# Attention values in lent PSUM banks of a feed-forward product, and softmax inverses spread in place, in a fused Linformer kernel

## The chip, the cores and the metric

The kernel runs on one core of one Trainium2 chip. The metric is the device time of one execution in microseconds (us), as the median of several runs. Five engines work side by side and meet through semaphores: TensorE (PE in the profile; PEld are its weight loads), VectorE (DVE), ScalarE (ACT), GpSimd (POOL) and SyncE (SP), which issues most DMAs here.

## The reference

A Linformer attention is followed by a feed-forward layer with a squared relu. There are 8 batches, 8 heads, 1024 tokens, a head width of 64, and keys and values are projected along the tokens to length 64; the feed-forward layer has widths 512, 2048, 512.

```python
k_proj = np.einsum('ks,bhsd->bhkd', E, k)          # E, F: 64 x 1024
v_proj = np.einsum('ks,bhsd->bhkd', F, v)
scores = (1 / sqrt(64)) * q @ k_proj^T             # 1024 x 64 per head
attn   = softmax(scores)                           # over the 64
x      = attn @ v_proj, heads side by side         # 8192 x 512
h      = np.maximum(x @ w_in, 0.0)                 # 8192 x 2048
out    = (h * h) @ w_out                           # 8192 x 512, float32
```

## The kernel before, in words

**The feed-forward part.** A batch is cut into two chunks of 512 tokens. For each chunk both feed-forward products are computed with a Strassen scheme (Winograd's form): seven half-size products in place of eight, with sums of the inputs made beforehand (`sum_x`, `sum_h`, and the sums of the weights). The first product is worked off in four `Group`s (g = 0 to 3) per chunk. A group has seven steps in the order `p1, p5, p4` (of the group before), `p6, p2, p3, p7`, each of four matmuls of 256 columns, written at line 669. It uses the PSUM banks `bank0` to `bank3`: `first` is bank 1, `other` is bank 2, and `chain` is bank 3 for even g and bank 0 for odd g.

```python
self.first, self.chain = bank(n=turn["bank"] + 1), bank(n=turn["bank"] + 3 + self.g % 2)
```

`p1` fills `first`, and ScalarE copies it to `chain` (L694). `p6` adds to `chain`, `p2` adds to `first`, and a relu on ScalarE (L679) takes each out when it is complete; for `other` (after `p3`) and for `chain` after `p7` a relu of a sum on VectorE does it (`relu_sum`, L683). So `first` lies free from the relu after `p2` until the next group's `p1`, and the chain bank of the group before lies free from the relu after its `p4` until ScalarE's copy after the next group's `p1`.

The second product of the chunk before runs between these steps (`second_spread`, L583): one step of the first product, then one quantum of four matmuls of the second, in its own two banks. Its product 1 ends with a copy of one bank to the other on ScalarE (L599); one step has no quantum and the next has two.

**The attention part.** The attention of the next batches is planned into these steps. Heads go in pairs; there are four pairs a batch, pr = 0 to 3. All of attention shares one pair of PSUM banks (`ps_att`, from `att_psum`). Per pair of heads:

- `scores` (L339): two matmuls of 512 columns, then an exponential on ScalarE (L353) to `expT`.
- `sums_spread` for two pairs at once (L392): eight matmuls on 64x32 tiles of the array with ones as weights; then ScalarE makes the inverse as exp(-ln(sum)) (L396, L397) in the tile `inv`. Each sum stands in 32 partitions, and the scaling needs it in 64. DMAs on SyncE (L403) copy it, 32 partitions of 4 KB each, to two places of a tile `rs` per pair of heads: eight DMAs in all. `inv` and `rs` come from a pool of three buffers.
- `values` (L415): four matmuls of 512 columns on the four 64x64 tiles of the array, into the two halves of `ps_att`; then VectorE multiplies each half by `rs` into `xT` (L419). `xT` is the input of the first product, and `sum_x` makes its sums.

**What sets the order.** TensorE's order is written out by hand: `run` counts steps, and `at` or `on` hangs a stage of attention behind a step. Steps count from 1; a chunk has 28, a batch 56, and `t = 56 * (b - 1) + 28` is the end of the first chunk of batch b, so that t+1 is `p1` of group 0 of its second chunk, t+6 is `p3` and t+7 `p7` of group 0, t+8 `p1` of group 1, t+20 `p3` of group 2, and t+22 `p1` of group 3. At t+6 there is no quantum of the second product, and at t+7 there are two. The other engines follow the order in which a scheduler places their instructions; `tc.issue_after(x)` puts an instruction behind x in it. The load of Q for the batch after next (GpSimd, L89) waits for the scaling of pair 1.

Of the kernel before, what the change touches and what calls it, by code (L numbers as in the profile page):

```python
# [9 lines left out]
P = 128  # L10
F32 = mybir.dt.float32
BF16 = mybir.dt.bfloat16
AF = mybir.ActivationFunctionType
# [6 lines left out]
def kernel(  # L20
# [11 lines left out]
    nc = tc.nc  # L32
# [12 lines left out]
    TCH = S // 2  # L45
# [15 lines left out]
    soft_pool = ctx.enter_context(tc.tile_pool(name="soft", bufs=3))  # L61
# [5 lines left out]
    turn = {"att": 0, "bank": 0, "step": 1, "pairs": 2}  # L67

    lent = ctx.enter_context(ExitStack())
# [5 lines left out]
    def att_psum(shape=(P, 2, TCH), dtype=F32):  # L75
        turn["att"] += 1
        return pair_psum(turn["att"] % turn["pairs"], shape, dtype)

    def bank(shape=(P, 512), dtype=F32, n=None):
        if n is None:  # L80
            turn["bank"] += turn["step"]
            n = turn["bank"]
        return psum.tile(list(shape), dtype, tag=f"bank{n % 4}", name="ps_bank")
# [48 lines left out]
    for j, (lo, hi) in enumerate(W_IN_PIECES):  # L132
        t = wpool.tile([P, NCB, (hi - lo) * P], BF16, name=f"w_in_{lo}")
# [7 lines left out]
    for j in range(WP):  # L141
        t = wpool.tile([P, fn, DM], BF16, name=f"w_out_{j}")
# [89 lines left out]
    class Attention:  # L232
# [153 lines left out]
        def sums_spread(self, pr):  # L386

            ps = att_psum()
            for j in range(2):
                for o, par, a, r in VALUE_QUADS:  # L390
                    c = 32 * (2 * a + j)
                    nc.tensor.matmul(  # L392
                        ps[c:c + 32, par], lhsT=ones[r, 0:32], rhs=self.e[pr + j][r, a], start=True, stop=True
                    )
            inv = soft_pool.tile([P, 2, TCH], F32, tag="rs", name="inv")
            nc.scalar.activation(inv[:], ps[:], AF.Ln)  # L396
            nc.scalar.activation(inv[:], inv[:], AF.Exp, scale=-1.0)  # L397
            for j in range(2):
                rs = soft_pool.tile([P, 2, TCH], F32, tag="rs", name="rs")
                for a in range(2):  # L400
                    have = 32 * (2 * a + j)
                    for to in (64 * a, 64 * a + 32):
                        nc.sync.dma_start(rs[to:to + 32], inv[have:have + 32])  # L403
                self.rs[pr + j] = rs

        def values(self, pr, spare=False):

            e, rs = self.e.pop(pr), self.rs.pop(pr)
            if spare:
                ps_x = [bank(), bank()]  # L410
            else:
                ps = att_psum()
                ps_x = [ps[:, par] for par in range(2)]
            for o, par, a, r in VALUE_QUADS:
                nc.tensor.matmul(  # L415
                    ps_x[par][o], lhsT=self.vp[r, 2 * pr + a, :], rhs=e[r, a], start=True, stop=True
                )
            for par in range(2):
                self.done = nc.vector.tensor_tensor(  # L419
                    out=self.xT[:, pr, :, par], in0=ps_x[par].rearrange("p (c t) -> p c t", c=2),  # L420
                    in1=rs[:, par].rearrange("p (c t) -> p c t", c=2), op=ALU.mult,
                )


        def chunk_scores(self, c, g):
# [234 lines left out]
    class Group:  # L660
# [19 lines left out]
            self.square(kh, a)  # L680

        def relu_sum(self, kh, a, ps, more):
            nc.vector._custom_dve(TENSOR_ADD_SAT, out=self.out(kh, a), in0=ps[:], in1=more[:], s0=3.0e38, s1=0.0)  # L683
            self.square(kh, a)

        def square(self, kh, a):
# [38 lines left out]
    with tc.manual_schedule(engines={PE}):  # L725
# [33 lines left out]
        def at(step, fn, *args, **kwargs):  # L759
            plan.setdefault(step, []).append(lambda: fn(*args, **kwargs))  # L760
# [110 lines left out]
        def on(step, b, name, *args):  # L871
            at(step, lambda: getattr(atts[b], name)(*args))
# [5 lines left out]
        for b in range(B - 1):  # L878
            t = 56 * (b - 1) + 28
            if b:  # L880
                on(t + 1, b + 1, "scores", 3)
                on(t + 3, b + 1, "sums_spread", 2)
                on(t + 7, b + 1, "values", 0)
                on(t + 10, b + 1, "values", 1)
                on(t + 20, b + 1, "values", 2)
                on(t + 23, b + 1, "values", 3)
                at(t + 24, lambda b=b: chunk[b + 1, 0].sum_x())
            at(t + 51, lambda b=b: chunk[b + 1, 1].sum_x())
            if b + 2 < B:
                if b:  # L890
                    on(t + 11, b + 2, "load_q", lambda b=b: atts[b + 1].done)
                on(t + (26 if b else 32), b + 2, "transpose_q_dma")
                on(t + (28 if b else 36), b + 2, "project")
                on(t + (30 if b else 37), b + 2, "transpose_k_dma")
                if b + 3 < B:
                    at(t + (32 if b else 37), begin, b + 3)
                    on(t + (32 if b else 37), b + 3, "load_kv", lambda b=b: atts[b + 2].kT_done)
                on(t + (44 if b else 45), b + 2, "scores", 0)
                on(t + (47 if b else 48), b + 2, "scores", 1)
                on(t + (50 if b else 51), b + 2, "sums_spread", 0)  # L900
                on(t + (53 if b else 54), b + 2, "scores", 2)
# [34 lines left out]
```

The softmax here doesn't subtract the row's maximum and nothing guards it: scores larger than these inputs give would overflow.

## Time and profile before

| | before |
|---|---|
| median of 5 runs | 473.03 us (472.68 to 475.01) |
| profiled execution, its own time | 473.03 us |
| its span, first to last instruction | 471.2 us |
| TensorE, VectorE, ScalarE busy | 465.3, 348.1, 297.7 us |
| one period of 56 steps (a batch) | 55.33 us |
| matmul pieces at L669 and L583 on the chain that ended last | 37% and 36% |
| DMAs `rs<-inv` (L403) | 96, of 128 KB each, median 2.3 us to landing |

A row of a timeline has the start in us from the span's start, the length in us, engine, source line, operation, the tile written and the tiles read; for matmuls then the tile of the array and the moving operand's shape, the number of like instructions in a row, and in brackets the idle time before and what ended it. A matmul's length goes up to its modelled end, so that runs of matmuls overlap in these rows; the distance between starts is the time that TensorE spends.

### The profile page before, as it was taken

To read this page: it belongs to the slowest core of one execution; us is meant where nothing else is said; L and a number is where in the kernel's file an instruction comes from. 1 tells how busy PE (TensorE), PEld (TensorE's weight loads), DVE (VectorE), ACT (ScalarE), POOL (GpSimd) and SP (SyncE) were. 2 spreads that over 40 slices of the span, in tenths; PEclk is the share of its full clock that TensorE was granted. 3 is DMA by queue.
4 is the path that set the end of the run, shared out by engine and by line. 5 is a ranking of instruction groups with operands and counts; after the bars stand their busy time and mean duration, and the time that the engine had idled before them with its cause. 6 is when DMAs were issued, how large, how long until landed. Compare 5 with 4: busy or idle time off the path is not lost.

```text
span 471.2 us, 10124 instructions
## 1 busy us (share of the span) xinstructions
PE 465.3 (99%) x4141; PEld 367.2 (78%) x4141; DVE 348.1 (74%) x596; ACT 297.7 (63%) x484; POOL 34.0 (7%) x47
## 2 busy tenths in 40 slices
PE   8999999999999999999999999999999999999997
PEld 4544677788888787887888888888878878888886
DVE  2469985876968779667895679777796778968571
ACT  3488595887467863687556775568736875565641
POOL 7430100100010000100001000100000000000000
PEclk9999999999999999999999999999999999999999
DMA  9999998995879578785979849695692154101012
GB/s 181 201 205 206 161 199 187 173 223 111 170 151 210 144 134 202 127 171 130 175 183 145 170 105 177 154 195 156 108 209 89 32 132 106 68 24 68 24 69 89
DMA packets 85743, 67.90 MB, mean 144 GB/s; under 512 B 34368, under 2 KB 82240, under 8 KB 85696
## 3 DMA queue, kind: packets, MB, share of 16 engines
q0 software_dynamic: 32208, 29.23, 41.0%
q1 hardware_dynamic: 53488, 38.02, 30.2%
q8 instruction: 32, 0.52, 0.5%
q14 instruction: 15, 0.12, 0.1%
HBM read 59.24 MB, written 16.78 MB: 161 GB/s over the span
## 4 chain that ended last, share of the span: by engine, by line
PE 97%; DMA 1%; DVE 1%; issue 0%; ACT 0%; POOL 0%; DVEq 0%; POOLq 0%
PE ps_bank L669 37%; PE ps_second L583 36%; PE ps_bank L502 6%; PE ps_bank L562 4%; PE ps_att L339 3%; PE ps_att L270 3%; PE ps_att L415 2%; PE ps_second L562 1%; DMA Q_sb<-in_q_dram 1%; PE ps_att L392 1%; PE ps_bank L314 1%; PE ps_att L349 1%; PE ps_att L345 1%; PE ps_att L289 0%; PE ps_bank L220 0%; DVE qT L318 0%
## 5 line engine op out<-in xcount | busy, mean ns | idle before, releaser
L154 DVE TENSOR_TENSOR h<-h 128x1024 bf16<-128x1024 bf16 (+1 forms) x170 | 105.4, 646 | 43.9 <-ACT h L679 38.7
L669 PE MATMUL ps_bank<-x_sum,w_in_sum 128*128 128x256 bf16 x672 | 101.1, 273 | 0.0
L669 PEld LDWEIGHTS <-w_in_sum 128*128 128x128 bf16 x896 | 85.3, 98 | 19.0 <-issue 6.3
L583 PEld LDWEIGHTS <-h 128*128 128x128 bf16 x896 | 87.4, 98 | 10.8
L683 DVE CUSTOM_DVE_ANT_0 h<-ps_bank,u 128x512 bf16<-128x512 f32 x112 | 73.8, 685 | 16.3 <-PE ps_bank L669 12.1
L557 ACT COPY u<-ps_bank 128x512 f32<-128x512 f32 x115 | 68.0, 591 | 24.9 <-PE ps_bank L669 23.7
L694 ACT COPY ps_bank<-ps_bank 128x512 f32<-128x512 f32 x56 | 32.0, 571 | 81.5 <-PE ps_bank L669 81.5
L679 ACT ACTIVATE h<-ps_bank 128x512 bf16<-128x512 f32 x112 | 67.9, 607 | 16.7 <-PE ps_bank L669 15.8
L669 PEld LDWEIGHTS <-w_in 128*128 128x128 bf16 x672 | 64.2, 98 | 14.6 <-issue 5.2
L583 PEld LDWEIGHTS <-s 128*128 128x128 bf16 x672 | 65.7, 98 | 7.7
L669 PE MATMUL ps_bank<-xT,w_in 128*128 128x256 bf16 x448 | 67.3, 273 | 0.0
L583 PE MATMUL ps_second<-w_out_sum,s 128*128 128x256 bf16 x448 | 67.3, 273 | 0.0
L583 PE MATMUL ps_second<-w_out_sum,h 128*128 128x256 bf16 x448 | 67.1, 273 | 0.0
L583 PE MATMUL ps_second<-w_out,h 128*128 128x256 bf16 x448 | 64.7, 273 | 0.0
L419 DVE TENSOR_TENSOR xT<-ps_att,rs 128x512 bf16<-128x512 f32 x48 | 30.9, 685 | 13.7 <-PE ps_att L415 13.7
L353 ACT ACTIVATE expT<-ps_att 128x1024 bf16<-128x1024 f32 x32 | 33.1, 1034 | 5.3 <-PE ps_att L339 5.0
L154 DVE TENSOR_TENSOR o_sb<-ps_second,u 128x512 f32<-128x512 f32 x29 | 19.9, 685 | 19.3 <-PE ps_second L583 13.6
L669 PE MATMUL ps_bank<-x_sum,w_in 128*128 128x256 bf16 x224 | 33.7, 273 | 0.0
L669 PE MATMUL ps_bank<-xT,w_in_sum 128*128 128x256 bf16 x224 | 33.6, 273 | 0.0
L583 PE MATMUL ps_second<-w_out,s 128*128 128x256 bf16 x224 | 33.6, 273 | 0.0
L502 PE MATMUL ps_bank<-xT,w_in 128*128 128x512 bf16 x128 | 29.2, 380 | 0.0
L557 ACT COPY u<-ps_second 128x512 f32<-128x512 f32 x30 | 17.6, 585 | 11.6 <-PE ps_second L583 9.3
(96 smaller groups left out, 461.8 us busy)
## 6 DMA issues: line engine op xcount, KB each, us to landing
out_dram<-o_sb SPq DMA_DIRECT2D x63, 256.0 KB, 2.5
rs<-inv SPq DMA_DIRECT2D x96, 128.0 KB, 2.3
K_sb<-in_k_dram POOLq DMA_DIRECT2D x7, 1024.0 KB, 10.1
V_sb<-in_v_dram POOLq DMA_DIRECT2D x7, 1024.0 KB, 14.7
Q_sb<-in_q_dram POOLq DMA_DIRECT2D x6, 1024.0 KB, 12.0
w_out<-in_moe_w_out_dram POOLq DMA_DIRECT2D x4, 512.0 KB, 15.9
Q_sb<-in_q_dram POOLq DMA_DIRECT2D x4, 256.0 KB, 11.0
V_sb<-in_v_dram POOLq DMA_DIRECT2D x2, 512.0 KB, 11.0
```

The source lines that it names most:

```text
L154: return nc.vector.tensor_tensor(out=o, in0=x, in1=y, op=op)
L270: nc.tensor.matmul(ps[LO, 0], lhsT=ET[:, i, :], rhs=self.K[:, :, i, :], start=f, stop=l)
L353: self.done = nc.scalar.activation(e[:], ps[:], AF.Exp, scale=SCALE)
L419: self.done = nc.vector.tensor_tensor(out=self.xT[:, pr, :, par], in0=ps_x[par].rearrange("p (c t) -> p c t", c=2), in1=rs[:, par].rearran ...
L502: nc.tensor.matmul(ps[:], lhsT=w_in_blk(cb, fb), rhs=self.xT[:, cb, self.c].rearrange("p a t -> p (a t)"), start=(cb == 0), stop=(cb == NC ...
L557: nc.scalar.copy(u[:], ps)
L562: nc.tensor.matmul(ps[:, i * HM:(i + 1) * HM], lhsT=self.h_form(n, fb)[:, i * P:(i + 1) * P], rhs=w_out_form(n, fb), start=fresh and fb == ...
L583: nc.tensor.matmul(ps[:, i * HM:(i + 1) * HM], lhsT=self.h_form(n, fb)[:, i * P:(i + 1) * P], rhs=w_out_form(n, fb), start=fresh and i == ...
L669: nc.tensor.matmul(ps[:, j * HC:(j + 1) * HC], lhsT=w_in_form(n, cb, 2 * self.g + j), rhs=self.chunk.x_form(n, cb), start=fresh and j == 0 ...
L679: nc.scalar.activation(self.out(kh, a), ps[:], AF.Relu)
L683: nc.vector._custom_dve(TENSOR_ADD_SAT, out=self.out(kh, a), in0=ps[:], in1=more[:], s0=3.0e38, s1=0.0)
L694: nc.scalar.copy(self.chain[:], self.first[:])
```

## The change

In the six batches b = 1 to 6 of the plan (they compute the attention of batches 2 to 7):

- The sums of pairs 2 and 3 move from t+3 to t+6, and the values of pair 0 from t+7 to t+6, behind them.
- The values of pair 2 stay at t+20; the matmuls of pair 3's values move from t+23 to t+20, behind them, and their scaling to t+21.
- The values of pairs 0 and 2 go to bank 1 and bank 0 of the first product (`values_lent`); those of pairs 1 and 3 stay in `ps_att`. VectorE's relu-sum after `p7` of that group is put behind the scaling of the lent banks.
- The inverse is made in the first of the two `rs` tiles, so that there is no tile `inv`: four DMAs fill the second tile, then two complete the first in place, six instead of eight.

```diff
-            inv = soft_pool.tile([P, 2, TCH], F32, tag="rs", name="inv")
-            nc.scalar.activation(inv[:], ps[:], AF.Ln)
-            nc.scalar.activation(inv[:], inv[:], AF.Exp, scale=-1.0)
-            for j in range(2):
-                rs = soft_pool.tile([P, 2, TCH], F32, tag="rs", name="rs")
+            rs = [soft_pool.tile([P, 2, TCH], F32, tag="rs", name="rs") for _ in range(2)]
+            nc.scalar.activation(rs[0][:], ps[:], AF.Ln)
+            nc.scalar.activation(rs[0][:], rs[0][:], AF.Exp, scale=-1.0)
+            for j in (1, 0):
                 for a in range(2):
                     have = 32 * (2 * a + j)
                     for to in (64 * a, 64 * a + 32):
-                        nc.sync.dma_start(rs[to:to + 32], inv[have:have + 32])
-                self.rs[pr + j] = rs
-
-        def values(self, pr, spare=False):
-
-            e, rs = self.e.pop(pr), self.rs.pop(pr)
-            if spare:
-                ps_x = [bank(), bank()]
-            else:
+                        if j or to != have:
+                            nc.sync.dma_start(rs[j][to:to + 32], rs[0][have:have + 32])
+                self.rs[pr + j] = rs[j]
+
+        def values_products(self, pr, lent):
+            ps_x = [bank(n=turn["bank"] + n)[:] for n in (1, 4)] if lent else None
+            if not lent:
                 ps = att_psum()
                 ps_x = [ps[:, par] for par in range(2)]
+            e = self.e.pop(pr)
             for o, par, a, r in VALUE_QUADS:
                 nc.tensor.matmul(
                     ps_x[par][o], lhsT=self.vp[r, 2 * pr + a, :], rhs=e[r, a], start=True, stop=True
                 )
+            self.ps_x[pr] = ps_x
+
+        def scale(self, pr):
+            ps_x, rs = self.ps_x.pop(pr), self.rs.pop(pr)
             for par in range(2):
                 self.done = nc.vector.tensor_tensor(
                     out=self.xT[:, pr, :, par], in0=ps_x[par].rearrange("p (c t) -> p c t", c=2),
                     in1=rs[:, par].rearrange("p (c t) -> p c t", c=2), op=ALU.mult,
                 )
+            return self.done
+
+        def values(self, pr):
+            self.values_products(pr, False)
+            self.scale(pr)
+
+        def values_lent(self, pr):
+            self.values_products(pr, True)
+            turn["lent"] = self.scale(pr)
...
         def relu_sum(self, kh, a, ps, more):
-            nc.vector._custom_dve(TENSOR_ADD_SAT, out=self.out(kh, a), in0=ps[:], in1=more[:], s0=3.0e38, s1=0.0)
+            with ExitStack() as order:
+                if (kh, a) == (1, 1) and "lent" in turn:
+                    order.enter_context(tc.issue_after(turn.pop("lent").ins))
+                nc.vector._custom_dve(TENSOR_ADD_SAT, out=self.out(kh, a), in0=ps[:], in1=more[:], s0=3.0e38, s1=0.0)
             self.square(kh, a)
...
                 on(t + 1, b + 1, "scores", 3)
-                on(t + 3, b + 1, "sums_spread", 2)
-                on(t + 7, b + 1, "values", 0)
+                on(t + 6, b + 1, "sums_spread", 2)
+                on(t + 6, b + 1, "values_lent", 0)
                 on(t + 10, b + 1, "values", 1)
-                on(t + 20, b + 1, "values", 2)
-                on(t + 23, b + 1, "values", 3)
+                on(t + 20, b + 1, "values_lent", 2)
+                on(t + 20, b + 1, "values_products", 3, False)
+                on(t + 21, b + 1, "scale", 3)
                 at(t + 24, lambda b=b: chunk[b + 1, 0].sum_x())
```

## The prediction

> **What bounds the kernel now.** I read the busy shares first, then the granted clock, the waits of TensorE, and TensorE's own timeline through one batch.
>
> ```profile
> PE 465.3 (99%) x4141; PEld 367.2 (78%) x4141; DVE 348.1 (74%) x596; ACT 297.7 (63%) x484; POOL 34.0 (7%) x47
> PEclk9999999999999999999999999999999999999999
> PE ps_bank L220 <- DVE zeros L123: 1.2, 1, 1.2
> PE ps_bank L211 <- DVE e_bf L727: 0.5, 1, 0.5
> PE ps_att L339 <- DVE kT L301: 0.4, 2, 0.2
> PE ps_bank L278 <- ACT K_sb L728: 0.3, 1, 0.3
> 151.83:207.16 55.33, 55.33 (x506) 45.46 (x505) 42.96 (x73) 35.58 (x60) 2.62 (x3) 1.00 0.79 161
> ```
>
> TensorE is busy for 99% of the span at full clock. Its four listed waits come to 2.4 us, all before 61 us, outside the stretches that the change touches. The last line is one period of 56 steps: 55.33 us, TensorE busy throughout. So whatever TensorE time disappears moves the end, unless a wait takes its place. The change removes no matmul; it can gain only where matmuls stand closer together.
>
> ```profile
> 161.92 0.60 PE L583 MATMUL ps_second<-w_out,h 128*128 128x256 bf16 x4
> 162.36 0.60 PE L669 MATMUL ps_bank<-xT,w_in_sum 128*128 128x256 bf16 x4
> 162.80 0.60 PE L669 MATMUL ps_bank<-x_sum,w_in_sum 128*128 128x256 bf16 x4
> 163.26 1.03 PE L583 MATMUL ps_second<-w_out,h 128*128 128x256 bf16 x8
> 164.22 0.41 PE L415 MATMUL ps_att<-expT,vp 64*64 64x512 bf16 x4
> 164.57 0.61 PE L669 MATMUL ps_bank<-xT,w_in 128*128 128x256 bf16 x4
> ```
>
> Each row is a run of matmuls: start, length, tile of the array. Full-array runs of four start 0.437 us apart. The eight from 163.26 need 0.875, so they end streaming at 164.13; values start at 164.22, and the next full-array run at 164.57. The four values matmuls (four different 64x64 quarters, all four inside 0.41 us where one alone takes 0.40) therefore cost 0.44 us of TensorE.
>
> ```profile
> 184.35 0.40 PE L270 MATMUL ps_att<-K_sb,ET 128*64 128x512 bf16 x1
> 184.59 0.38 PE L270 MATMUL ps_att<-K_sb,ET 128*64 128x512 bf16 x1
> 184.81 0.38 PE L270 MATMUL ps_att<-K_sb,ET 128*64 128x512 bf16 x1
> ```
>
> These are 512-column matmuls that follow each other with no change of tile shape: 0.24 us to the second, 0.22 to the third. So of the 0.44 about 0.215 is streaming, and 0.22 is paid for changing shape twice: 0.11 us a change. The sums (64x32) cost the same: 160.60 less the end of streaming before them (159.73 + 0.437) is 0.43.
>
> **The change, part by part.** It acts in six batches (b = 1 to 6; the trace has 24 blocks of values and 12 of sums).
>
> *Place A, t+6.* The sums of pairs 2 and 3 move from t+3 to t+6 and the values of pair 0 from t+7 to t+6, right behind them. Two lone blocks have four changes of shape; adjacent they have three: into 64x32, to 64x64, out. The trace has no change between two small shapes. Bounds: it is free (gain 0.22), or as dear as a way out and in (gain 0). I take one ordinary change, 0.11, as both small shapes cost alike against the full array: gain 0.11.
>
> [...]
>
> *Place B, t+20.* Values of pair 3 move from t+23 next to values of pair 2. Same shape, so two changes go: 0.22, less up to 0.02 for the first follower (0.24 instead of 0.22 above). I take 0.21.
>
> *A small wait.* At 163.26 the run starts 0.03 late (162.80 + 0.437 = 163.23): it waits for ScalarE's copy of the second bank (L599, 162.62 to 163.21). With the sums behind it, the last matmul of t+5 ends 0.43 earlier and the copy at about 162.8, while TensorE needs it at about 163.6. Gain 0.03.
>
> *The lent banks.* Values of pairs 0 and 2 now write the bank of `first` and the bank that odd groups use as `chain`. Three new meetings follow.
>
> (1) Values wait for ScalarE's relu of product 2 on bank 1. At B product 2 ends streaming at 175.07; relu ran 175.27 to 175.87 and values would start at 176.47: 0.6 spare. At A the relu comes at 161.7 to 162.3, values at 162.79: 0.5 spare. Cost 0.
>
> (2) Product 1 of the next group, two steps on, waits for the first half of the scaling. The order of the built program has this wait on the first of the two VectorE multiplies. VectorE starts 0.47 us after the first values matmul (164.69 against 164.22), a half takes 0.69, and a released TensorE starts 0.04 later.
>
> ```profile
> 176.35 0.68 DVE L683 CUSTOM_DVE_ANT_0 h<-ps_bank,u 128x512 bf16<-128x512 f32 x1
> 176.95 1.28 DVE L419 TENSOR_TENSOR xT<-ps_att,rs 128x512 bf16<-128x512 f32 x2
> 162.02 0.69 DVE L154 TENSOR_TENSOR s<-h,s 128x1024 bf16<-128x1024 bf16 x1
> 163.10 1.29 DVE L683 CUSTOM_DVE_ANT_0 h<-ps_bank,u 128x512 bf16<-128x512 f32 x2 [0.39 <-PE ps_bank L669]
> ```
>
> At B the first half is done at 176.95 + 0.69 + 0.04 = 177.68; product 1 stood at 177.70 and comes 0.22 later, behind the second block: 0.24 spare. (In one batch VectorE starts this scaling 0.25 later: nothing spare, nothing lost.) At A: product 3 streams from 161.92, sums from 162.45, values from 162.79; the relu-sum of product 3 follows the subtraction that ends at 162.71 and takes until about 163.35; first half done about 164.05, given back 164.09. Product 1 comes after product 7 and the two second-product runs of t+7, at 162.79 + 0.34 + 0.437 + 0.875 = 164.44: 0.35 spare. Cost 0, cover thin at both. ScalarE's copy into the other lent bank comes after product 1 (165.05 at A) and the second half ends at 164.7. Cost 0.
>
> (3) The relu-sum of product 7 now stands behind the scaling on VectorE: at A it ends at about 165.3, where product 4 wants the bank at 166.2. At B nothing moves (it stands there already). The scaling of pair 3 gets earlier, from 180.0 to about 179.4. Cost 0.
>
> *Spreading in place.* Per pair of pairs 6 DMAs of 128 KB replace 8, on SyncE, which is not on the path: no gain. But pair j=0's two now wait until j=1's have read their source, and in the program the sixth stands behind an output store. Who waits for it is VectorE's scaling, behind that TensorE. Rows of the second batch: the exponential ends at about 165.0, DMAs 1 to 4 go out from 165.1 to 167.0 (0.63 each) and land 2.3 later, the last at 169.2. DMA 5 goes at 168.0, then the store, and DMA 6 at 169.3. Just then GpSimd issues the load of Q (169.34, now about 169.2), and that matters:
>
> ```profile
> L403 SPq DMA_DIRECT2D rs<-inv x4: 513/588/590, 166.0 to 167.9; - x4
> DMA to landing us min/median/max: 2.2/2.3/2.3
> ...
> L403 SPq DMA_DIRECT2D rs<-inv x3: 590/590/592, 169.6 to 170.9; - x3
> DMA to landing us min/median/max: 5.9/7.1/7.2
> ```
>
> Ahead of that load a spread lands in 2.3 us, behind it in 5.9 to 7.2. DMA 6 lands between 171.6 and 176.5, nearest the 5.9 row: 175.2. The scaling at B wants it at 176.8. Cost 0 to 0, with 0.3 to 1.6 spare. At A the same spread was made nine steps before: DMA 6 is held by a store until about 159.6 and lands at about 162, wanted at 163.3. In the first batch alone the landing takes 2.5 to 4 us and may be up to 0.6 late: I put 0.1 us for it, once.
>
> *Sum.* (0.11 + 0.21 + 0.03) x 6 = 2.1, less 0.1: 2.0 us. The profiled execution took 473.03 us, of which 471.2 span, and it is also the median of the five runs. Forecast 473.03 - 2.0 = 471.0 us. With A at its ends, 470.3 to 471.7.
>
> **The rivals.** *Slower: the sixth spread lands late.* The mechanism is the wait that spreading in place adds, beside the Q load, in five batches (the last has no such load). The output store behind the Q load took 7.9 us to land at 171.99, and 9.5 in the first batch. If DMA 6 fares like these, say 8.9 us, it lands at 178.2, the scaling is 1.4 late, 0.24 is spare, product 1 stops for 1.15: 5 x 1.15 - 2.0 = +3.8, 476.8 us. It decides from a landing 8.2 us after issue (a stop of 0.4 a batch eats the gain). Against: DMA 6 goes out within 0.1 us of the load, and the spread issued 0.28 behind it took 5.9.
>
> *About the same: the lent bank comes back late.* If product 1 waits in earnest at both places, 0.2 to 0.6 us a batch together (the whole second half would be 0.35 at B and 0.27 at A), the time is 472.2 to 474.6, most likely 473. For: spare times of 0.24 and 0.35 on an engine busy 78% of the period. Against: both are worked out from rows that repeat from batch to batch.
>
> *Half of what it says: the change between small shapes is as dear as two.* (0.21 + 0.03) x 6 - 0.1 = 1.3 gained, 471.7 us.
>
> *More: that change is free.* 2.7 gained, 470.3 us.
>
> **How the numbers follow.** Forecast 0.60, free change 0.10, dear change 0.10, bank late 0.13, spread late 0.07. About 0.3% or 1.4 us is what a measurement here can tell from no change, so faster means below 471.6. Faster: 0.58 of the forecast, 0.10, and a little of the dear case, 0.70; slower: the spread and the bad end of the late bank, 0.10; the rest, 0.20, is within. The range runs from 470.2 to 473.0: below it lies a part of the free case, above it the slower cases.
>
> **What would show it.** Period of 56 steps 54.98 instead of 55.33. At t+20 eight values matmuls with the second four 0.21 to 0.24 behind the first, the pair costing 0.65 us; at t+6 sums and values costing 0.76 (0.87: the dear case, 0.65: the free one). No wait of TensorE on VectorE's multiply ahead of product 1; if one stands there, and VectorE in turn sat idle until a spread DMA landed, the slower rival holds. If the period shrinks and the time does not, the path lies elsewhere and I misread the first view.

## The result, and the profile after

| | before | after |
|---|---|---|
| median, runs | 474.17 us, 63 runs (472.45 to 476.25) | 472.36 us, 37 runs (470.36 to 475.20) |
| ratio after / before | | 0.9973, 95% interval 0.9964 to 0.9982 |
| profiled execution, span | 473.03, 471.2 us | 471.65, 469.9 us |
| one period of 56 steps | 55.33 us | 54.95 us |
| start to the first projection of the second period (L270) | 79.82 us | 80.79 us |

The kernel became faster by 0.27% (0.18 to 0.36%), which is 1.3 us by the ratio (and between the means) and 1.8 us between the medians; 2.0 was predicted. The runs of before are not the five that the forecast started from: 25 of the 63 lie from 472.45 to 473.57 and 38 from 473.98 to 476.25, with nothing between the two groups.

The page after, busy shares, then the waits of TensorE, then the stretch from one marked projection to the next (L270):

```profile
PE 464.3 (99%) x4141; PEld 368.2 (78%) x4141; DVE 347.2 (74%) x596; ACT 298.3 (63%) x484; POOL 34.0 (7%) x47
```
```profile
PE ps_bank L220 <- DVE zeros L123: 1.2, 1, 1.2
PE ps_bank L211 <- DVE e_bf L741: 0.5, 1, 0.5
PE ps_att L339 <- DVE kT L301: 0.2, 1, 0.2
PE ps_bank L298 <- ACT kp L259: 0.2, 1, 0.2
```
```profile
129.63:184.58 54.95, 54.95 (x505) 45.57 (x505) 42.81 (x72) 35.70 (x59) 2.62 (x3) 1.00 0.76 148
```

TensorE is still the bound at 99%, none of its listed waits belongs to the change, and the period has become 0.38 us shorter with TensorE busy throughout.

TensorE's timeline after, place A and then place B (start, length, line, tile of the array). Lines of after: sums L392, values L413, first product L680, second product L594.

```profile
162.51 0.60 PE L680 MATMUL ps_bank<-xT,w_in_sum 128*128 128x256 bf16 x4
163.03 0.41 PE L392 MATMUL ps_att<-expT,ones 64*32 64x512 bf16 x8
163.38 0.41 PE L413 MATMUL ps_bank<-expT,vp 64*64 64x512 bf16 x4
163.72 0.61 PE L680 MATMUL ps_bank<-x_sum,w_in_sum 128*128 128x256 bf16 x4
164.16 1.04 PE L594 MATMUL ps_second<-w_out,h 128*128 128x256 bf16 x8
165.04 0.60 PE L680 MATMUL ps_bank<-xT,w_in 128*128 128x256 bf16 x4
...
176.40 0.60 PE L594 MATMUL ps_second<-w_out_sum,h 128*128 128x256 bf16 x4
176.93 0.41 PE L413 MATMUL ps_bank<-expT,vp 64*64 64x512 bf16 x4
177.17 0.39 PE L413 MATMUL ps_att<-expT,vp 64*64 64x512 bf16 x4
177.49 0.61 PE L680 MATMUL ps_bank<-x_sum,w_in_sum 128*128 128x256 bf16 x4
```

At A the run before the sums ends streaming at 162.51 + 0.437 = 162.95, and the next full-array run starts at 163.72: the two blocks cost 0.77 us, where two lone ones cost 0.43 + 0.44. At B it is 177.49 - (176.40 + 0.437) = 0.65, with the second block 0.24 behind the first. The eight second-product matmuls start at 164.16, right at the end of the streaming before them (163.72 + 0.437): the 0.03 us of waiting for the copy is gone.

VectorE's timeline after, at the two places:

```profile
163.25 0.69 DVE L697 CUSTOM_DVE_ANT_0 h<-ps_bank,u 128x512 bf16<-128x512 f32 x1
163.85 1.28 DVE L421 TENSOR_TENSOR xT<-ps_bank,rs 128x512 bf16<-128x512 f32 x2
...
176.81 0.68 DVE L697 CUSTOM_DVE_ANT_0 h<-ps_bank,u 128x512 bf16<-128x512 f32 x1
177.41 1.28 DVE L421 TENSOR_TENSOR xT<-ps_bank,rs 128x512 bf16<-128x512 f32 x2
```

The first half of the scaling (L421) gives the lent bank back at 163.85 + 0.69 + 0.04 = 164.58 at A, 0.46 us before product 1 (165.04), and at 178.14 at B, where product 1 starts at 178.37: 0.23 to spare.

So the period does what was predicted. Six shorter stretches should show 2.3 us in the profile (0.36 in the first, 0.38 to 0.44 in the four full periods, 0.39 in the tail); the spans differ by 1.4 (471.25 and 469.88). The rest is at the start. TensorE's timeline there, before and then after (L220 are matmuls on zeros that fill the wait for the first loads):

```profile
5.81 1.04 PE L220 MATMUL ps_bank<-zeros 128*128 128x512 bf16 x4
7.16 1.03 PE L278 MATMUL ps_bank<-K_sb,ET 128*64 128x256 bf16 x8 [0.31 <-ACT K_sb L728]
```
```profile
5.92 1.89 PE L220 MATMUL ps_bank<-zeros 128*128 128x512 bf16 x4
7.74 1.71 PE L278 MATMUL ps_bank<-K_sb,ET 128*64 128x256 bf16 x8
```

The same four matmuls take 1.89 instead of 1.04 us and the eight that follow 1.71 instead of 1.03. In the clock records of the traces full TensorE clock is granted from 4.55 us in the profile of before and from 9.11 us in that of after; the first projection of the second period comes 0.97 us later. 2.34 - 0.97 = 1.37 is the difference of the spans.

### The profile page after: what moved, and what is told of

It is laid out like the page before. It is cut to its first block, busy times and chain, and to the rows that moved or that the text cites. A ratio compares the mean times of both kernels' runs of the same rounds, so it can differ in the third digit from the quotient of the medians.

```text
span 469.9 us, 10095 instructions
## 1 busy us (share of the span) xinstructions
PE 464.3 (99%) x4141; PEld 368.2 (78%) x4141; DVE 347.2 (74%) x596; ACT 298.3 (63%) x484; POOL 34.0 (7%) x47
## 4 chain that ended last, share of the span: by engine, by line
PE 97%; DMA 1%; DVE 1%; ACT 0%; issue 0%; DVEq 0%
PE ps_bank L680 37%; PE ps_second L594 36%; PE ps_bank L513 6%; PE ps_bank L573 4%; PE ps_att L339 3%; PE ps_att L270 3%; PE ps_second L573 1%; PE ps_bank L220 1%; PE ps_att L392 1%; PE ps_bank L413 1%; DMA e_f<-in_E_dram 1%; PE ps_att L413 1%; PE ps_bank L314 1%; PE ps_bank L278 1%; PE ps_att L349 1%; PE ps_att L345 1%
## 5 line engine op out<-in xcount | busy, mean ns | idle before, releaser
L680 PE MATMUL ps_bank<-x_sum,w_in_sum 128*128 128x256 bf16 x672 | 101.1, 273 | 0.0
L680 PEld LDWEIGHTS <-w_in_sum 128*128 128x128 bf16 x896 | 85.3, 98 | 20.1 <-issue 7.4
L594 PEld LDWEIGHTS <-h 128*128 128x128 bf16 x896 | 87.5, 98 | 10.5
L680 PEld LDWEIGHTS <-w_in 128*128 128x128 bf16 x672 | 65.2, 98 | 12.1 <-issue 2.5
L594 PEld LDWEIGHTS <-s 128*128 128x128 bf16 x672 | 65.6, 98 | 7.7
L680 PE MATMUL ps_bank<-xT,w_in 128*128 128x256 bf16 x448 | 67.3, 273 | 0.0
L594 PE MATMUL ps_second<-w_out_sum,s 128*128 128x256 bf16 x448 | 67.2, 273 | 0.0
L594 PE MATMUL ps_second<-w_out_sum,h 128*128 128x256 bf16 x448 | 67.1, 273 | 0.0
L594 PE MATMUL ps_second<-w_out,h 128*128 128x256 bf16 x448 | 64.7, 273 | 0.0
L680 PE MATMUL ps_bank<-xT,w_in_sum 128*128 128x256 bf16 x224 | 33.6, 273 | 0.0
L680 PE MATMUL ps_bank<-x_sum,w_in 128*128 128x256 bf16 x224 | 33.6, 273 | 0.0
L594 PE MATMUL ps_second<-w_out,s 128*128 128x256 bf16 x224 | 33.6, 273 | 0.0
L421 DVE TENSOR_TENSOR xT<-ps_att,rs 128x512 bf16<-128x512 f32 x24 | 15.4, 684 | 14.9 <-PE ps_att L413 14.9
```

The source lines that it names most:

```text
L421: self.done = nc.vector.tensor_tensor(out=self.xT[:, pr, :, par], in0=ps_x[par].rearrange("p (c t) -> p c t", c=2), in1=rs[:, par].rearran ...
L594: nc.tensor.matmul(ps[:, i * HM:(i + 1) * HM], lhsT=self.h_form(n, fb)[:, i * P:(i + 1) * P], rhs=w_out_form(n, fb), start=fresh and i == ...
L680: nc.tensor.matmul(ps[:, j * HC:(j + 1) * HC], lhsT=w_in_form(n, cb, 2 * self.g + j), rhs=self.chunk.x_form(n, cb), start=fresh and j == 0 ...
```

## The experiments

Theory 1: A, B and the small wait bring 0.38 us a period, near what was worked out, and the start takes a part that differs from run to run. Theory 2, its rival: something that the first profile of after does not show, a stop somewhere in the changed schedule, takes a part in other executions.

**The same start for both.** VectorE's first conversion waits for the last load of V, so that the work begins when the loads are done, and 70 matmuls on zeros run before it. The edit to each kernel:

```diff
-        load(V0[:, h], tokens(v, 0, h=h))
+        v_last = load(V0[:, h], tokens(v, 0, h=h))
...
-        nc.vector.tensor_copy(e_bf[:], e_f32[:])
+        held = nc.vector.tensor_copy(e_bf[:], e_f32[:])
+        tc.add_manual_dep(held.ins, v_last.ins.name, ..., reason="held start")
...
-        warm(8)
+        warm(70)
```

> The kernel before with a held start: 70 dummy matmuls in place of 8, and the first real work waits for the last load of V (landed at 18 us in both profiles), so that TensorE works at full clock and all first loads are there when it begins. It is longer than the kernel before by the hold, some 12 to 14 us, and serves as the base for held_after. Theory 1 (the missing gain lies in the start, in when TensorE gets its full clock): its times spread by under 0.6 us, where the kernel before spreads over 472.4 to 476.3. Theory 2 (the missing gain lies in the 56-step periods): its times spread as before. Period 55.33 us by both.

> The changed kernel with the same held start. Theory 1: shorter than held_before by 2.2 to 2.4 us (six periods of 0.38 us), with a spread under 0.6 us. Theory 2: shorter by 1.0 to 1.5 us, as in the profiled spans without the hold (471.2 and 469.9). Period 54.95 us by both.

Measured: 486.27 us (485.79 to 487.36) and 483.83 us (483.64 to 485.31), 2.4 apart; spans 484.8 and 483.5. Periods 55.34 and 54.95. But the first stretch between marked projections is 49.20 in the one and 50.58 in the other, where after had 48.84: TensorE stops for 1.74 us in the first batch. The executions did not lie within the 0.6 us that theory 1 asked for, but spread over 1.6 and 1.7 us; the profiled one of the changed kernel, with the stop, took 485.31 us, and the other three 483.64 to 483.86. The rival was real, and what follows is about that stop.

**After once more, unchanged, and with two more matmuls on zeros at the start:**

```diff
-        warm(8)
+        warm(10)
```

> The changed kernel as it is, again. Theory 1: period 54.95 us again, and the time until the first projection of a batch (54.39 us in the profile before, 55.36 in the profile after) anywhere in about 54.3 to 56 us, following the moment at which the granted clock becomes full. Theory 2: the period or the number of stops in it differs from the first profile's. Time 470.4 to 474.

> The changed kernel with 10 dummy matmuls in place of 8 at the start, so that TensorE has no idle time between 4.6 and 5.2 us. Theory 1: the full clock comes by 8 us at the latest, the first transposes of Q start as soon as Q lands (8.6 us in the profile before, where the changed kernel's profile has them at 9.6), and the median falls by about 1 us to about 471.3 with a smaller spread. Theory 2: no change, about 472.4.

Measured: 471.87 us (470.49 to 475.41, 12 runs), ratio 0.9957 [0.9937, 0.9978], and 471.55 us (470.78 to 473.16, 11 runs), ratio 0.9951 [0.9935, 0.9967]. The longer warm-up did narrow the spread, as theory 1 had it, but both profiles have the stop in the first batch, 1.61 and 0.93 us. TensorE's timeline of after once more, at place A of the first batch, then VectorE's, then SyncE's and the answer for the one DMA issued at 108.36:

```profile
111.34 1.04 PE L594 MATMUL ps_second<-w_out,h 128*128 128x256 bf16 x8
113.83 0.60 PE L680 MATMUL ps_bank<-xT,w_in 128*128 128x256 bf16 x4 [1.45 <-DVE xT L421]
```
```profile
113.08 1.29 DVE L421 TENSOR_TENSOR xT<-ps_bank,rs 128x512 bf16<-128x512 f32 x2 [1.97 <-DMA rs<-rs]
```
```profile
102.70 4.93 SPq L403 DMA_DIRECT2D rs<-rs  x5
107.72 0.53 SPq L588 DMA_DIRECT2D out_dram<-o_sb  x1
108.36 0.51 SPq L403 DMA_DIRECT2D rs<-rs  x1
```
```profile
DMA to landing us min/median/max: 4.6/4.6/4.6
```

Read from the bottom: the sixth spread DMA goes out at 108.36, behind an output store, and lands at 113.0; VectorE sat 1.97 us for it; product 1 (L680) needs the lent bank and sat for VectorE. After 111.34 + 0.875 = 112.22 TensorE has nothing until 113.83. In the first profile of after that DMA went out at 105.24, landed 2.6 us later, and nobody waited. The first four DMAs go out at the same moment in both (7.9 to 6.0 us before the values), but in this batch the load of V runs beside them; it lands at 103.2 in the first profile and at 106.1 in this one, and the second of the four lands at 103.95 and 107.07. The fifth, which overwrites what the first two read, goes out 0.05 us after that, and the sixth 1.24 us after the fifth, with the store between. That is 1.0 of the 3.0 us by which the sixth lands later against the values. The other 2.0 us is its own time, 4.6 instead of 2.6 us, though V had landed 2.3 us before it went out. Over the twelve profiles with six DMAs it took 2.6 us in five and 3.8 to 4.7 in seven. In the seven a 16 KB packet of the queue that the profile calls instruction (q8) starts while it is under way, in four of the five none does; no run varied this, so why the sixth is slow stays open. This profile also has the clock drop to half from 7.53 to 14.35 us, so that its marked projection comes at 82.92.

The stop goes with that landing in every profile of kernels that make the inverse of pairs 0 and 1 in pair 0's tile and need it at t+6:

| kernel | sixth DMA lands, from the first values matmul of A | stop of TensorE |
|---|---|---|
| after | 0.56 us earlier | 0 |
| after_again2 (below) | 0.01 earlier | 0 |
| one_shape (below) | 1.00 later | 0.18 |
| after_warm | 1.76 | 0.93 |
| a_only (below) | 1.88 | 1.04 |
| after_again | 2.45 | 1.61 |
| held_after | 2.58 | 1.74 |

Stop = landing - 0.83, within 0.02 us in the five that stop; up to 0.83 us is covered.

**Other tile first.** If that chain of DMAs is the cause (theory 3 of the expectations), it helps to make the inverse of pairs 0 and 1 in pair 1's tile: pair 0's is then filled by the first four, and pair 1's is wanted four steps later.

```diff
-            nc.scalar.activation(rs[0][:], ps[:], AF.Ln)
-            nc.scalar.activation(rs[0][:], rs[0][:], AF.Exp, scale=-1.0)
-            for j in (1, 0):
+            keep = 1 if pr == 0 else 0
+            nc.scalar.activation(rs[keep][:], ps[:], AF.Ln)
+            nc.scalar.activation(rs[keep][:], rs[keep][:], AF.Exp, scale=-1.0)
+            for j in (1 - keep, keep):
```

> The changed kernel, with the inverse of pairs 0 and 1 made in pair 1's tile instead of pair 0's: the first four spread DMAs then complete pair 0's tile, and the two in place, which must wait for them, belong to pair 1, whose scaling comes four steps later. Theory 3 (a good part of the missing gain is one stop in the first batch, where TensorE's product 1 waits for VectorE's scaling of pair 0 and that for the sixth spread DMA: 0.9 to 1.7 us in three of the last four profiles): no stop, the stretch from the first to the third marked projection is 74.27 us as in the first profile after (25.43 + 48.84), and the median falls by 0.8 to 1.4 us below the changed kernel's 471.9 to 472.4. Rival (that stop is made by the profiling alone, and the loss is the start's): the median stays at 471.9 to 472.4.

The same with `warm(10)`, and before with `warm(10)`:

> The same with 10 dummy matmuls at the start in place of 8. Theory 3 with theory 1: both losses are gone, all times within 470.2 to 471.2 us, median about 470.6. Rival: as after_warm, median 471.5.

> The kernel before with 10 dummy matmuls in place of 8. Theory 1 (the two groups of the kernel before's times, near 472.8 and near 474.3, come from the moment of the full clock at the start): one group, near 472.8 to 473.2, so that swap_warm is 2.3 us shorter (six periods of 0.38). Theory 2 (the groups come from elsewhere): two groups as before, median near 474.

Measured: 471.78 us (470.98 to 471.88, 5 runs), ratio 0.9951 [0.9937, 0.9964]; 470.97 (470.40 to 471.12, 5 runs), 0.9932 [0.9920, 0.9945]; and for before 473.06 (472.84 to 473.85, 11 runs), 0.9981 [0.9968, 0.9993]. The sixth DMA still lands 2.55 and 2.21 us after the values begin, and TensorE does not stop: first stretch 48.84 in both, periods 54.95. The 11 runs of before with the longer warm-up lie in one group where the plain kernel has two, so its upper group belongs to the start. Between the last two kernels, which share their start, the spans differ by 2.3 us, the medians by 2.1 and the means by 2.3.

**Place A alone**, with the spread in place; B undone in the changed kernel:

```diff
-                on(t + 20, b + 1, "values_lent", 2)
-                on(t + 20, b + 1, "values_products", 3, False)
-                on(t + 21, b + 1, "scale", 3)
+                on(t + 20, b + 1, "values", 2)
+                on(t + 23, b + 1, "values", 3)
```

> Place A alone: sums and values of pair 0 at t+6 with lent banks and spreading in place; values of pairs 2 and 3 at t+20 and t+23 in the attention banks as before. By the prediction's terms the period is 55.33 - 0.11 - 0.03 = 55.19 us. If the change between the two small shapes were as dear as two it would be 55.30, if it were free 55.08. The stop in the first batch (theory 3) may stand in the profile, so that the time lies between 0.8 us below and 1 us above the kernel before's.

Measured: 473.90 us (471.86 to 476.77, 10 runs), ratio 1.0001 [0.9981, 1.0020]. Period 55.21, 0.13 less than before: A's 0.10 and the 0.03 of the copy. Over six batches that is 0.8 us, and the stop in the first batch, 1.04 in its profile, is as large.

**Spreading in place alone, and place B with it.** A undone in the changed kernel; in the first of the two B is undone too, as above:

```diff
-                on(t + 6, b + 1, "sums_spread", 2)
-                on(t + 6, b + 1, "values_lent", 0)
+                on(t + 3, b + 1, "sums_spread", 2)
+                on(t + 7, b + 1, "values", 0)
```

> Spreading in place alone; all stages at their steps and in their banks as before. Theory 3 (the late sixth DMA costs only through a lent bank): period 55.33 to 55.40, no stop of TensorE in the first batch even where VectorE's scaling of pair 0 waits for a DMA, median as the kernel before's within 0.4 us. Rival (spreading in place costs by itself): a stop of TensorE in the first batch, median up by 0.5 us or more.

> Place B alone: values of pair 2 lent and pair 3 behind them at t+20; sums at t+3 and values of pair 0 at t+7 in the attention banks as before; spreading in place. By the prediction's terms the period is 55.33 - 0.21 = 55.12 us. No stop in the first batch by theory 3 (scaling of pair 0 is one step later and no lent bank waits for it), so the median is 1.2 to 1.4 us below the kernel before's. Rival (the lent bank comes back late at B): the period stays above 55.2.

Measured: 480.86 us (480.69 to 482.68), ratio 1.0162 [1.0133, 1.0191], and 481.86 us (481.84 to 482.35), ratio 1.0178 [1.0150, 1.0205]. Neither theory had this. The waits of TensorE, spreading alone, and ScalarE's timeline there, then that of before:

```profile
PE ps_second L594 <- ACT ps_second L610: 6.5, 10, 0.8
```
```profile
161.97 1.02 ACT L396 ACTIVATE rs<-ps_att 128x1024 f32<-128x1024 f32 x1
162.89 0.58 ACT L568 COPY u<-ps_bank 128x512 f32<-128x512 f32 x1
163.35 1.07 ACT L397 ACTIVATE rs<-rs 128x1024 f32<-128x1024 f32 x1
164.31 0.60 ACT L690 ACTIVATE h<-ps_bank 128x512 bf16<-128x512 f32 x1
164.79 0.61 ACT L610 COPY ps_second<-ps_second 128x512 f32<-128x512 f32 x1
```
```profile
162.62 0.59 ACT L599 COPY ps_second<-ps_second 128x512 f32<-128x512 f32 x1
163.13 1.02 ACT L396 ACTIVATE inv<-ps_att 128x1024 f32<-128x1024 f32 x1
164.19 1.06 ACT L397 ACTIVATE inv<-inv 128x1024 f32<-128x1024 f32 x1
```

In the kernel before, the logarithm (L396) comes behind the copy of the second bank (L599). Without `inv` and with the sums still at t+3, the scheduler puts logarithm and exponential ahead of that copy (L610), and TensorE stops for 0.99 us a batch waiting for it (and in four batches for 0.5 us more at the same copy in the other chunk). Moving the sums to t+6 puts the order right again, so the parts of this change cannot be priced one by one with the schedule as it falls. Place B with in-place spreading has a second wait:

```profile
PE ps_second L594 <- ACT ps_second L610: 5.0, 6, 0.8
PE ps_bank L680 <- DVE xT L421: 2.2, 4, 0.8
```

That is the slower rival of the prediction: there the sixth DMA of the second spread goes out 0.7 to 0.97 us behind the load of Q and takes 5.8 to 7.7 us to land, in four of six batches so late that TensorE stops for 0.37 to 0.96 us. With spreading alone it is as late (in four batches 1.15 to 1.33 us after the values begin), and VectorE's scaling waits 0.7 to 0.9 us, but no bank is lent there and TensorE has no stop at B: the late landing costs through the lent bank.

**One change of shape less.** The sums by four 64x64 matmuls (sums of the second pair of heads left out), so that sums and values share a tile shape:

```diff
-            for j in range(2):
-                for o, par, a, r in VALUE_QUADS:
-                    c = 32 * (2 * a + j)
-                    nc.tensor.matmul(
-                        ps[c:c + 32, par], lhsT=ones[r, 0:32], rhs=self.e[pr + j][r, a], start=True, stop=True
-                    )
+            for o, par, a, r in VALUE_QUADS:
+                nc.tensor.matmul(
+                    ps[64 * a:64 * a + 64, par], lhsT=ones[r, 0:64], rhs=self.e[pr][r, a], start=True, stop=True
+                )
```

> The changed kernel with the sums made by four matmuls on 64x64 tiles in place of eight on 64x32; it leaves out the sums of the second pair of each two, which is scaled by the first pair's inverse. If the change from 64x32 to 64x64 at t+6 costs as much as any change of shape, the pair of blocks there costs 0.65 us instead of 0.776 and the period is 54.95 - 0.12 = 54.83 us; if it is free, both are unchanged (54.95).

Measured, a single execution: 472.31 us, span 470.5. Its timeline at A:

```profile
161.79 0.60 PE L678 MATMUL ps_bank<-xT,w_in_sum 128*128 128x256 bf16 x4
162.32 0.41 PE L390 MATMUL ps_att<-expT,ones 64*64 64x512 bf16 x4
162.56 0.39 PE L411 MATMUL ps_bank<-expT,vp 64*64 64x512 bf16 x4
162.88 0.61 PE L678 MATMUL ps_bank<-x_sum,w_in_sum 128*128 128x256 bf16 x4
```

162.88 - (161.79 + 0.437) = 0.65 instead of 0.77, and the one undisturbed period is 54.83 instead of 54.95: the change from 64x32 to 64x64 costs 0.12 us, beside the 0.11 worked out for a change to or from the full array. That there are four matmuls instead of eight is not what saves it: alone, the eight on 64x32 and the four on 64x64 take 0.34 and 0.35 us in before (160.26 to 160.60, 164.22 to 164.57). The rival of the free change falls. The total did not gain: in two batches the sixth DMA went out 0.91 and 1.04 us behind the load of Q, took 7.6 and 7.3 us, and TensorE stopped for 0.76 and 0.93 us at B.

**Side by side: eight DMAs again, B alone without in-place spreading, after, and the other tile first.** The first is the changed kernel with the loop of before; the second has that loop too, and A undone as above:

```diff
-            rs = [soft_pool.tile([P, 2, TCH], F32, tag="rs", name="rs") for _ in range(2)]
...
+            inv = soft_pool.tile([P, 2, TCH], F32, tag="rs", name="inv")
...
+                        nc.sync.dma_start(rs[to:to + 32], inv[have:have + 32])
```

> The changed kernel (places A and B as they are), but the inverse made in a tile of its own again and spread by eight DMAs that need not wait for one another. If the missing part of the gain is the stop of TensorE in the first batch, and that stop comes from spreading in place (the sixth DMA waits for the fifth), then: no stop of TensorE on VectorE's multiply in the first batch, first stretch between marked projections 48.8 us (after_again2: 49.7 to 50.4), later periods 54.95, time 0.5 to 1.3 us below after_again2 and level with swap2. If the missing part is only the later start (the clock), the first stretch has no stop in either of the two and their times agree within 0.4 us.

> Place B alone (values of pair 3 behind those of pair 2 in lent banks), with the spread, the sums and all else as before. The prediction's price of two changes of tile shape: period 55.33 - 0.22 = 55.11 us, no stops, 1.3 us below before over six batches. If lending the bank costs product 1 a wait (the rival of the late bank), the period is between 55.2 and 55.4, with a wait of TensorE on VectorE's multiply ahead of product 1 after t+20.

> The changed kernel once more, as the measure for the others of this call. Periods 54.95 us; the first stretch 48.84 without a stop or 49.7 to 50.5 with one of 0.9 to 1.7 us on VectorE's multiply in the first batch, depending on when its sixth DMA lands beside the loads of K and V; 1.3 to 2.5 us below before.

> The changed kernel with the inverse of pairs 0 and 1 made in the tile of pair 1, so that pair 0's tile, which is wanted first, is filled by the first four DMAs. No stop in the first batch, first stretch 48.84, periods 54.95, 0.5 to 1.3 us below after_again2 if the stop is what is missing; level with after_again2 if only the start is.

| | median (range, runs) | ratio to before, interval | first stretch | next period |
|---|---|---|---|---|
| before | 474.29 (472.71 to 475.48, 35) | | 49.20 | 55.33 |
| old_spread | 472.82 (472.04 to 474.36, 12) | 0.9980 [0.9965, 0.9995] | 50.29 | 54.95 |
| b_old | 472.49 (471.41 to 473.58, 10) | 0.9969 [0.9953, 0.9985] | 48.97 | 55.09 |
| after_again2 | 472.56 (470.53 to 474.72, 12) | 0.9975 [0.9956, 0.9995] | 48.84 | 54.95 |
| swap2 | 470.89 (470.41 to 474.56, 12) | 0.9954 [0.9934, 0.9974] | 48.84 | 54.95 |

(The stretches of before are from its own profile.)

*old_spread* was a miss for my theory. It has no stop at A, as expected, but one of 1.46 us at B of the first batch. Its timelines of TensorE, VectorE and ScalarE, and the answer for the first four DMAs of that spread:

```profile
125.31 0.60 PE L680 MATMUL ps_bank<-xT,w_in 128*128 128x256 bf16 x4 [1.29 <-DVE xT L421]
```
```profile
124.57 1.29 DVE L421 TENSOR_TENSOR xT<-ps_bank,rs 128x512 bf16<-128x512 f32 x2 [1.59 <-DMA rs<-inv]
```
```profile
110.65 1.02 ACT L396 ACTIVATE inv<-ps_att 128x1024 f32<-128x1024 f32 x1 [1.81 <-DVE xT L421]
```
```profile
DMA to landing us min/median/max: 2.2/4.6/8.0
```

`inv` is a third tile of a pool of three; the tile it gets is, by its waits, pair 0's, which the scaling at t+6 still reads, right beside the sums. So the logarithm waits 1.81 us for VectorE, the DMAs go out 3.5 us later than in after (from the values of A), the third and fourth behind the load of Q (0.6 and 1.23 us), and they take 6.8 and 8.0 us. Spreading in place is therefore not a mere saving of two DMAs: it also spares the logarithm this wait. TensorE paid for the wait in this batch; the four periods behind it are 54.95, 54.95, 55.00 and 55.11, and the median is not below that of after_again2, as expected, but level with it.

*b_old*: first stretch 0.23 shorter than before, the four periods 0.25, 0.25, 0.24 and 0.10, the tail 0.25, with no wait on a lent bank. B was priced at 0.21; alone it brings at least that in five of six. *swap2* against *after_again2*: 1.7 us lower in the median, 1.2 in the mean (95% interval about 0.1 to 2.3). The profile of after_again2 is one without a stop, equal to that of swap2 within 0.1 us of span (468.7 and 468.8), so the profiles don't show how often the other 11 runs stopped. Swap kernels did not stop in any of three profiles, after and its variants in five of seven. They beat before and, in the median, after.

## Why the prediction was right or wrong

- **The bound, places A and B, the small wait: right.** TensorE at 99%, A 0.10 (0.11 predicted), B 0.22 (0.21), the wait 0.03 (0.03). The period fell by 0.38 us; I had 0.35 (54.98). With A alone (a_only) it fell by 0.13, with B alone (b_old) by 0.25, together 0.38. Most of what B has beyond 0.22 is a small wait that I did not see: in the batch's other chunk the eight second-product matmuls follow the run ahead of them after 0.465 us instead of 0.484, and they do so in b_old too.
- **The lent banks at no cost: right** in every full period of after; spare 0.46 and 0.23 us where 0.35 and 0.24 were worked out.
- **The load of Q: right for this kernel, by little.** The sixth DMA went out from 0.27 us ahead of the load to 0.70 behind it and landed in 2.4 to 5.2 us; I had reckoned with 5.9. In three neighbouring kernels (b_only, one_shape, old_spread) the DMAs in question left 0.6 to 1.2 us behind the load, and the slower rival came true.
- **"I put 0.1 us for it, once": the step that failed.** I took the landing in the first batch from rows of before (2.5 to 4 us), where none of the eight DMAs waits for another, and allowed 0.6 us. In place, two landings stand one behind the other with a store between, the first stretched beside the load of V, the second taking 2.6 to 4.7 us: the sixth landed up to 2.6 us after the values began, and the stop was 0 to 1.74 us, present in five of seven profiles. With the other tile first, where product 1 does not wait for that chain, the means are lower by 0.8 to 1.2 us (below); the sum had 0.1. The bound should have been two landings long; and the cover, VectorE's free time, was gone, since product 1 now waits on the lent bank. My own sign of the slower rival, that wait on VectorE's multiply with VectorE idle for a spread DMA, came, but in the first batch and not beside the load of Q.
- **The level: wrong by 1.1 us.** The profiled execution, 473.03, was taken for the median; 63 runs give 474.17. I said that the profiled execution is the median of the five runs shown and did not weigh that one of the five was 475.01. Before's upper group goes away with a longer warm-up, so it is a matter of the start, and the profile of before (full clock from 4.55 us) had one of the early ones.
- **The dear and the free change of shape** are both excluded by A's 0.77 us and by one_shape. The 0.11 us for this change was an estimate; one_shape shows 0.12.
- **The chance of 0.70 for more than 0.3%.** The work in the period would have given 2.3 / 474.2 = 0.5%. What the first batch took left 0.27%, less than the 0.3% that I called the least to be told from no change.

How the 1.0 us between 2.3 and the ratio's 1.3 divides between stop and start, the runs say in part. The means fall from before to after by 1.3 us with the plain start and by 1.5 with the longer warm-up in both (before_warm, after_warm); to the kernel with the other tile first they fall by 2.3 us with either start. The pairs with and without that wait on the chain differ by 1.0 (after, swap), 0.8 (after_warm, swap_warm) and 1.2 us (after_again2, swap2), each known to 0.4 to 1.1 us (after_warm ran on another chip than its partners). So most of the missing 1.0 us is the first-batch stop, and the start moves both kernels alike.

Open: how often runs that were not profiled stopped, and what makes the sixth DMA take 3.8 to 4.7 us in some of them.

## What to carry to other kernels

When a buffer is lent from a busy engine's chain to a side job, that job's inputs come onto the path (here a stop of up to 1.74 us, in held_after): work out the landing of every DMA behind it, in the first iteration too, where the initial loads run beside it. Spreading in place saves a tile and makes the last copies wait for the first ones (in after_again the fifth went out 0.05 us after the second had landed); so make the result in the tile that is wanted last. Price against many runs of before, not the one that was profiled, and look at the scheduler's order on every engine before taking a part of a change for separable.

## What the runs showed of the hardware

- Around the loads of Q (1 MB, GpSimd), over all 17 profiles and the spread DMAs of 128 KB that SyncE issued within 8 us of one: those over 0.3 us ahead of the load land in 2.2 to 3.8 us (median 2.3, 396 of them), those within 0.3 us of it in 2.3 to 6.0 (81), those 0.3 to 0.75 us behind it in 4.1 to 7.4 (20), and those 0.9 us or more behind it in 5.7 to 8.2 (62, median 7.4). In these profiles about one microsecond of order went with up to five of landing (medians 2.3 and 7.4).
- The clock at the start differs by run: full from 4.43 to 10.02 us in the traces with the start of 8 or 10 matmuls, and once (after_again) full from 4.11, half from 7.53 and full again from 14.35. In three profiles of the same kernel (after_again2, after, after_again), with full clock to the end of the span from 4.52, 9.11 and 14.35 us, the marked projection came at 79.63, 80.79 and 82.92 us; in the last of them TensorE also waited 1.4 us for the first conversion of K.
